# Sliding-window attention with a mixture of attention experts: a mask added by TensorE, loads in halves, expert outputs turned by transfers, and a new list of steps

## The chip, the cores and the metric

The kernel runs on one core of one Trainium2 chip. The metric is the device time of one execution in microseconds (us). Of three runs of the kernel before, the median is 242.83 us (240.96 to 242.97).

## The reference

```python
# attention: B=8 batches, H=8 heads, S=576 positions, D=64
scores = scale * np.matmul(q, k.transpose(0, 1, 3, 2))
mask = np.abs(pos[:, None] - pos[None, :]) <= 32
attn_out = softmax(np.where(mask, scores, -1e9)) @ v
x = attn_out.transpose(0, 2, 1, 3).reshape(B, S, 512)
# mixture: E=4 experts, Hd=64, the best two by gate for each position
logits = x @ w_gate                      # softmax weights w over the best two
for e in range(4):
    q, k, v = x @ wq[e], x @ wk[e], x @ wv[e]
    a = softmax(where(causal, -1e9, scale * q @ k.T))
    ye = a @ v @ wo[e]
    out += (w of e, or 0) * ye
```

All inputs and the output are float32.

## The kernel before

Everything is written as short steps, and the string `ORDER` lists them in the order in which they are issued. A step's name is an operation, then its batch `b` and further digits; `:a`, `:v`, `:g` name the engine of a copy (ScalarE = ACT, VectorE = DVE, GpSimd = POOL), `@` the PSUM banks. Each engine runs its instructions strictly in that order, and waits by semaphores for what another engine or a transfer delivers. Nothing is scheduled at run time, so the list decides what stands behind what. There are three buffers (`NAT`) for loaded q and k tiles, two for v and two for the transposed tiles of each group.

Attention, for each batch and each group `g` of four heads:

- `lq`, `lk` load q and k, `lv` loads v, all from the queue of SyncE (SP), except q or k steps marked `:f`, which ACT issues. Each load carries a dependency on the last TensorE (PE) instruction that stands before it in the list (`load`), so it isn't issued before that one is done.
- `tq`, `tk` turn q and k by 32 x 32 blocks on DVE (`turn`); `vc` copies v into the second alignment that the windows need.
- `sc` computes half of the windowed scores (columns 0 to 287 or 288 to 575), each 64 keys against the queries of their window, in blocks `BLK`; `ex` takes the exponential from PSUM into `A` (ACT).
- `mk` multiplies `A` by the 0/1 band `MASK`, so that what lies outside the window is 0. All 64 are on POOL.
- `av` multiplies by v, with a column of ones for the sums; `un` divides (reciprocal and multiply on DVE) into `XN`.

Mixture, for each batch:

- `xt` turns `XN` on PE by an identity matrix, `xf` copies it out of PSUM, `xb` casts to bf16.
- `ga`, `gt`, `ge`, `gm`, `gu` compute the gate and the weights of the best two experts.
- `pp`, `pe` project to q and k of a pair `j` of experts, `pv`, `ve` to v.
- `ps`, `xe`, `se` compute the causal scores by chunks 0 to 3 (`CHUNKS`), their exponential (ACT) into `ATE`, and the causal zeroes on the diagonal blocks (POOL).
- `po` multiplies by v, `oe` scales by gate and sum (DVE) into `OE`.
- `pt` turns `OE` on PE: five matmuls of 128 x 128 with the bf16 identity, into a bank; `ot` copies the bank to `OTT`.
- `py` multiplies `OTT` by the output weights, `ye` copies to `Y`, `st` stores.

`zz` steps are four matmuls of zeroes that keep PE running. `s_` steps set constants up. `cw` and `lw` load and cast weights.

The program runs batch `b`'s mixture among batch `b+1`'s and `b+2`'s attention. In line L179 (`mm`) stand all matmuls, in L182 (`turn_pe`) all of PE's turns, in L171 and L173 (`copy`) all copies, in L294 the DVE turns, in L339 `ex`, in L343 `mk`, in L513 and L515 `xe`, in L518 `se`, in L551 to L553 `oe`, in L185 the loads.

Of the kernel before, what the change touches and what calls it, by code (L numbers as in the profile page):

```python
# [24 lines left out]
NOE = 2  # L25

ORDER = """
    lq011:f lq012:e lk011:e lk012:e s_warm tq011:e tq012:e tk011:e lq000:e s_ones lk000:e s_zero tk012:e tq000:e
# [4 lines left out]
    av03@4 ex1011@2 lw11 mk1011:g cw10:g av04@0 lk200:e un03@4 un04@0 lq200:e xt00@2 tq110:e xf00:a@2 xt02@0 xt01@4
    sc111@62 xf02:a@0 mk1010:g xf01:a@4 xb01:g xb02:g lv10 tk200:e xb00:a cw00:a ex1110@6 sc110@04 ex1101@4 cw11:g
    lv13 ex1111@2 pp000@6 pp001@4 lw01 pe000:a@6 mk1101:g mk1111:g mk1000:g pe001:v@4 ex1100@0 pp011@2 tq200:e lv14
    ps001@6 lw2 xe001@6 ps002@0 ga0@4 xe002@0 sc200@60 pe011:a@2 lq210:e cw01:a pp010@2 gt0@4 ge0@4 vc11:g gm0@4
    mk1110:g gu0@4 av13@4 lv20 vc10:a lv23 ex2000@6 av12@6 ex2001@0 pe010:v@2 un13@4 ps013@2 xe013@2 mk1100:g cw2:g
    ps010@0 ps000@4 av10@2 xe010@0 av11@0 lk210:e xe000@4 pv01@4 un12@6 un10@2 ve01:a@4 ps003@6 av14@5 xe003@6 ps011@2
    xe011@2 lk300:e un11@0 ps012@0 xt11@6 xf11:a@6 un14@5 xt10@4 tq210:e xf10:a@4 xe012@0 sc201@26 tk210:e mk2001:g
    se002 se003 se001 xb11:g mk2000:g lv21 ex2011@6 lv22 lq300:e ex2010@2 xb10:g pv00@4 xt12@0 xf12:v@0 ve00:a@4  # L40
    sc211@62 sc210@04 mk2010:g se012 tk300:e lq310:e se010 mk2011:g ex2111@2 xb12:a lk310:e ga1@2 ex2110@6 ex2100@0
    pv10@6 gt1@2 ge1@2 pp101@0 lv24 ex2101@4 gm1@2 pp110@4 pe110:a@4 gu1@2 ve10:a@6 lv33 tq300:e pp111@2 mk2110:g
    mk2111:g pe111:a@2 pp100@4 pe101:v@0 lv34 lv32 sc300@06 pe100:a@4 vc21:g tk310:e vc20:g pv11@2 av23@4 ex3000@0 lw3
    av22@0 mk2100:g ex3001@6 mk2101:g av24@3 un23@4 un22@0 un24@3 ps103@6 ve11:a@2 se000 po00@4 ps113@0 oe00@4 xe103@6
    xe113@0 ps110@6 xe110@6 lk400:e ps102@2 xt21@0 xe102@2 pt00@4 ot00:a@4 xt22@5 tq310:e av20@6 un20@6 av21@2
    xf21:a@0 ps111@0 xf22:a@5 sc301@46 un21@2 xe111@0 ex3010@4 lq400:e sc311@20 ex3011@6 ex3111@0 xt20@4 mk3000:g
    se011 ex3110@2 se102 xb21:g se113 lv31 se013 tk400:e cw3:g xb22:g mk3010:g mk3001:g ps100@6 xf20:a@4 lk410:e
    ps101@0 xe100@6 zz4@2 po01@2 lq410:e oe01@2 xe101@0 sc310@46 ex3101@6 xb20:g se100 se103 ex3100@4 ps112@0 pp211@2
    xe112@0 pp201@6 lq500:e lv30 se101 tq400:e pt01@0 po10@4 pe211:a@2 pp210@2 ot01:v@0 pp200@0 pe201:v@6 oe10@4
    vc30:g se110 mk3110:g mk3011:g mk3111:g pe200:a@0 mk3100:g sc401@64 pe210:v@2 lk510:e sc400@20 lk500:e ex4011@4  # L50
    ex4001@0 ex4000@2 pv20@4 mk3101:g ps201@0 ex4010@6 vc31:g se112 mk4010:g tk410:e ps202@2 xe201@0 xe202@2 tq410:e
    ve20:v@4 ga2@6 gt2@6 ge2@6 av34@7 un34@7 ps212@0 xe212@0 lv44 gm2@6 py01@4 xt32@7 lv43 gu2@6 ye01:a@4 pv21@0
    ve21:a@0 xf32:v@7 av32@2 un32@2 py02@1 lv42 ye02:a@1 av33@4 lq510:e av31@6 un33@4 ps203@0 ps200@2 xe203@0 xe200@2
    un31@6 tk500:e xt31@4 xf31:a@4 sc411@06 xb32:g mk4000:g mk4001:g mk4011:g lv52 se203 av30@2 un30@2 ex4111@6 lv41
    sc410@46 xt30@2 xb31:a se111 ex4110@0 ex4101@6 tq500:e ex4100@4 py00@0 mk4100:g mk4110:g xf30:a@2 st01 lv40 po11@6
    ye00:a@0 lv50 sc500@42 xb30:a ex5001@2 mk4101:g vc40:g ga3@0 lv54 oe11@6 ex5000@4 ps213@6 xe213@6 lq600:e ps210@2
    tq510:e ps211@4 lv51 pt10@1 xe210@2 xe211@4 pp300@6 gt3@0 vc41:g pe300:a@6 pp301@2 tk510:e ge3@0 mk4111:g
    pe301:a@2 sc501@46 ex5010@4 gm3@0 av40@2 lq610:e gu3@0 un40@2 ex5011@6 ot10:a@1 av42@4 av43@6 un42@4 av41@0
    ps300@2 ps302@4 un43@6 st00 lk600:e xe300@2 lv53 xt41@6 un41@0 xe302@4 pt11@0 xf41:v@6 xt40@2 mk5011:g xf40:a@2
    ot11:a@0 av44@1 un44@1 sc510@46 se201 se213 mk5000:g sc511@20 lk610:e se210 se212 mk5010:g se202 mk5001:g se211  # L60
    ex5101@6 ex5100@4 py10@6 mk5100:g se300 xb40:g tk600:e se200 ex5110@2 py11@4 lk710:e ye10:a@6 lk700:e po21@2
    xt42@6 ex5111@0 xf42:a@6 pv30@0 ye11:a@4 tq600:e pp310@6 oe21@2 tk610:e xb42:a ve30:a@0 po20@4 oe20@4 xb41:a
    mk5111:g mk5110:g mk5101:g pe310:a@6 vc51:g sc600@20 ex6000@2 ex6001@0 tq610:e pp311@6 pp401@2 pe311:a@6 ps303@4
    ps312@0 xe312@0 xe303@4 st02 lv60 av54@6 vc50:g ga4@7 lv64 ps313@0 un54@6 pe401:a@2 ps311@4 ps301@2 py12@6 gt4@7
    xe313@0 xe311@4 lv62 st10 av50@0 ye12:v@6 st12 lv63 av52@4 xe301@2 un50@0 lv61 pv31@6 ge4@7 sc601@20 un52@4
    pp400@4 lq700:e ex6010@2 gm4@7 ex6011@0 pe400:a@4 ve31:v@6 pp410@2 ps403@0 gu4@7 lv72 ps400@6 se312 xe403@0
    ps401@4 xe400@6 av51@0 un51@0 lv71 pe410:a@2 av53@6 un53@6 ps310@2 tk700:e xe401@4 xt50@0 xt51@4 xe310@2 xt52@2
    xf50:a@0 xf52:v@2 pt21@3 pp411@6 xf51:a@4 ot21:v@3 lq710:e sc610@04 pe411:v@6 xb50:a xb51:a ps402@2 mk6011:g se303
    mk6000:g se302 se301 xb52:g pp501@6 ex6100@0 ex6101@4 pe501:a@6 pp500@0 se313 se311 se310 tq700:e pt20@4 pe500:a@0
    po31@6 ot20:a@4 xe402@2 mk6010:g oe31@6 lv70 po30@0 vc61:g ps413@4 lv73 xe413@4 ps412@2 xe412@2 vc60:a oe30@0  # L70
    sc611@64 tk710:e tq710:e mk6101:g mk6001:g pp510@2 ex6111@4 ex6110@6 pe510:a@2 pv40@0 ps502@4 mk6100:g mk6111:g
    mk6110:g xe502@4 sc701@62 ve40:v@0 ex7010@6 ex7011@2 av61@4 av63@6 py22@0 pv51@1 un61@4 un63@6 ve51:a@1 av60@2
    av62@4 ye22:a@0 ps411@6 un60@2 un62@4 ps410@0 ga5@2 gt5@2 st11 av64@3 un64@3 ps503@4 xe411@6 xe410@0 lv74 ps500@6
    xe503@4 pp511@0 ge5@2 xe500@6 pe511:a@0 py21@4 ye21:a@4 sc700@60 gm5@2 gu5@2 ex7000@6 ex7001@0 se411 sc711@24
    xt61@6 xf61:v@6 pt31@0 ot31:v@0 xt62@1 ex7111@4 se500 se412 ex7110@2 xt60@4 xf62:a@1 xf60:a@4 pv41@1 ve41:v@1
    sc710@26 mk7000:g se402 se410 se400 se401 xb61:g se403 py20@4 ye20:v@4 mk7111:g po40@0 st20 st21 st22 vc70:a
    ex7100@2 pt30@2 se413 mk7100:g mk7010:g ex7101@6 mk7101:g se503 xb60:g ps511@6 ps513@4 ga6@3 oe40@0 xb62:a xe511@6
    gt6@3 ps501@0 xe513@4 ps510@6 po41@4 xe501@0 ot30:v@2 pt40@2 xe510@6 pv50@0 oe41@4 pt41@4 pp611@6 ge6@3 gm6@3
    ot41:v@4 pp600@4 pe611:v@6 pe600:v@4 ve50:a@0 se510 se501 pp610@0 py31@6 mk7001:g se502 ot40:a@2 ye31:a@6 pp601@4
    pe610:v@0 gu6@3 po50@0 pe601:a@4 oe50@0 ps602@2 ps512@6 vc71:g mk7011:g xe512@6 av71@4 un71@4 av70@0 st31 ps601@6  # L80
    un70@0 se511 mk7110:g av74@4 un74@4 xe602@2 se512 se513 xe601@6 ps610@2 ps611@0 xe610@2 pv61@5 av73@6 un73@6
    xe611@0 py32@4 xt70@2 py30@0 po51@6 ye32:a@4 ye30:a@0 xt72@4 xf70:v@2 ve61:v@5 xf72:a@4 st32 ps612@2 oe51@6 py42@5
    av72@0 ps600@6 xe612@2 ye42:v@5 un72@0 xe600@6 ps613@4 xb72:a xe613@4 py41@2 ye41:v@2 st30 xt71@0 se610 xf71:a@0
    st41 pv60@6 xb70:g se600 se601 xb71:g py40@2 ps603@0 ve60:a@6 xe603@0 pp710@4 pe710:v@4 pt51@0 ye40:v@2 se602
    se603 ot51:a@0 pt50@1 ot50:a@1 po60@6 se611 pp711@4 st42 se613 se612 po61@0 pe711:a@4 ps713@2 ps712@4 oe60@6
# [557 lines left out]
```

## Time and profile before

| | |
|---|---|
| median of 3 runs | 242.83 us |
| profiled execution, its own time | 242.79 us |
| its span | 240.7 us |
| PE busy | 214.6 us |
| DVE busy | 170.4 us |
| POOL busy | 157.4 us |
| ACT busy | 155.1 us |
| mean of all transfers | 169 GB/s |

The span is from the first to the last profiled instruction of the execution. Busy time is the time in which at least one instruction of an engine ran. PE's busy time is not the same as PE at its peak, since the ends of pipelined matmuls are modelled. The chain of waits follows the work that ended last back to the start. A window's row gives its length, busy time and instruction count of PE, PE's weight loads, DVE, ACT and POOL, the granted clock, the share of the transfer engines and GB/s. A group's row gives busy time and mean nanoseconds of one, and then the idle time before it with what ended it. A float32 matmul or weight load leaves two records in the trace.

### The profile page before, as it was taken

The page shows a single profiled execution, that of the slowest core. Times are in us where ns is not written, and L with a number is a line of the kernel's source. Part 1 is how long each engine was busy: PE and PEld are TensorE (multiplying, and loading weights), DVE is VectorE, ACT ScalarE, POOL GpSimd, SP SyncE. Part 2 cuts the span into 40 slices and gives each one's busy share as a digit, 9 for nine tenths or more (in the row PEclk, how much of TensorE's full clock was granted, in tenths as well). Part 3 has the DMA queues.
Part 4 walks back from the last instruction along what each step waited for, and adds up shares of the span by engine and source line. Part 5 has one row for each costly group of instructions (what it writes and reads, how often), then busy time and mean ns, then how long its engine had stood idle before and what let it go on. Part 6 is the DMA issues. An engine that isn't in the chain of part 4 may idle for free.

```text
span 240.7 us, 12380 instructions
## 1 busy us (share of the span) xinstructions
PE 214.6 (89%) x5542; PEld 172.7 (72%) x5556; DVE 170.4 (71%) x351; ACT 155.1 (64%) x241; POOL 157.4 (65%) x193
## 2 busy tenths in 40 slices
PE   0496688899999899999899998999999999999980
PEld 0463576688888688688697976887978878786650
DVE  2967584878789669886976986669845766847660
ACT  2045346958476683869757874998588647757841
POOL 7069948956994899685969962499039993250500
PEclk9999999999999999999999999999999999999997
DMA  6696799766966286578685829826010510332375
GB/s 226 264 229 158 139 255 262 176 173 207 319 147 198 87 260 167 201 191 218 155 245 162 300 51 250 205 101 177 5 26 3 200 58 35 112 112 92 108 283 197
DMA packets 55157, 40.65 MB, mean 169 GB/s; under 512 B 45376, under 2 KB 46400, under 8 KB 55104
## 3 DMA queue, kind: packets, MB, share of 16 engines
q1 hardware_dynamic: 54960, 39.57, 56.7%
q8 instruction: 43, 0.70, 1.2%
q10 hardware_dynamic: 144, 0.29, 0.4%
q14 instruction: 10, 0.08, 0.1%
HBM read 30.42 MB, written 9.44 MB: 166 GB/s over the span
## 4 chain that ended last, share of the span: by engine, by line
PE 81%; DVE 8%; DMA 4%; issue 3%; ACT 2%; ACTq 0%; DVEq 0%
PE PS L179 72%; PE PS L182 8%; DMA kn<-in_k_dram 3%; DVE Tkn L294 3%; DVE Tqn L294 2%; DMA qn<-in_q_dram 2%; ACT ATE L513 1%; DVE OE L553 1%; DVE XN L371 1%; DVE PS L551 0%; DVE RC L370 0%; DVE QKE L173 0%; ACT Y L171 0%; DVE RG L552 0%; ACTq L638 0%
## 5 line engine op out<-in xcount | busy, mean ns | idle before, releaser
L343 POOL TENSOR_TENSOR A<-A,MASKP 128x576 f32<-128x576 f32 x64 | 89.3, 1411 | 24.4 <-ACT A L339 23.8
L179 PE MATMUL PS<-Tqn,Tkn 32*64 32x128 f32 (+3 forms) x2560 | 46.9, 277 | 16.0 <-DVE Tkn L294 11.2
L179 PEld LDWEIGHTS PS<-Tqn,Tkn 32*64 32x64 f32 x2560 | 40.7, 135 | 22.6 <-DVE Tkn L294 12.2
L339 ACT ACTIVATE A<-PS 128x576 f32<-128x576 f32 x64 | 38.6, 651 | 28.2 <-PE PS L179 25.8
L513 ACT ACTIVATE ATE<-PS 128x1024 bf16<-128x1024 f32 x48 | 47.5, 1026 | 11.0 <-PE PS L179 10.9
L518 POOL TENSOR_SCALAR_AFFINE_SELECT ATE<-ATE 128x256 bf16<-128x256 bf16 (+1 forms) x80 | 29.0, 382 | 28.2 <-ACT ATE L513 17.1
L294 DVE STREAM_TRANSPOSE Tkn<-kn 128x576 f32<-128x576 f32 (+1 forms) x34 | 37.3, 1176 | 8.5 <-DMA kn<-in_k_dram 6.8
L294 DVE STREAM_TRANSPOSE Tqn<-qn 128x576 f32<-128x576 f32 (+1 forms) x34 | 37.2, 1176 | 7.0 <-DMA qn<-in_q_dram 4.6
L179 PE MATMUL PS<-V,A 128*64 128x65 f32 (+1 forms) x1280 | 38.5, 222 | 0.6 <-ACT V L171 0.4
L179 PEld LDWEIGHTS PS<-V,A 128*64 128x64 f32 (+1 forms) x1280 | 35.9, 132 | 3.3 <-issue 1.0
L371 DVE TENSOR_TENSOR XN<-PS,RC 128x512 f32<-128x512 f32 x32 | 22.1, 691 | 1.1
L173 POOL CAST XTB<-XTF 128x1024 bf16<-128x1024 f32 (+1 forms) x18 | 12.4, 704 | 15.5 <-DVE XTF L173 8.4
L173 POOL COPY V<-V 64x2048 f32<-64x2048 f32 (+1 forms) x12 | 21.0, 1749 | 0.8 <-issue 0.2
L179 PE MATMUL PS<-WO,OTT 128*128 128x512 bf16 (+1 forms) x85 | 18.9, 342 | 0.9 <-DVE OTT L173 0.3
L171 ACT COPY XTF<-PS 128x1024 f32<-128x1024 f32 (+1 forms) x23 | 14.9, 699 | 6.9 <-PE PS L182 6.7
L182 PE MATMUL PS<-ident,XN 128*128 128x128 f32 x144 | 19.3, 277 | 0.0
L179 PE MATMUL PS<-WV,XTB 128*128 128x256 bf16 (+1 forms) x192 | 18.6, 256 | 0.2 <-ACT ATE L513 0.2
L171 ACT CAST QKE<-PS 128x576 bf16<-128x576 f32 x21 | 13.4, 643 | 7.5 <-PE PS L179 7.5
L179 PE MATMUL PS<-XTB,WK 128*128 128x288 bf16 x128 | 18.0, 286 | 0.1
L179 PE MATMUL PS<-QKE 64*128 64x64 bf16 (+4 forms) x192 | 17.0, 278 | 1.1 <-DVE QKE L173 1.1
L171 ACT COPY Y<-PS 128x1024 f32<-128x1024 f32 (+2 forms) x16 | 12.2, 778 | 8.8 <-PE PS L179 8.8
L179 PE MATMUL PS<-XTB,WQ 128*128 128x288 bf16 x128 | 17.9, 286 | 0.0
(71 smaller groups left out, 264.1 us busy)
## 6 DMA issues: line engine op xcount, KB each, us to landing
qn<-in_q_dram SPq DMA_DIRECT2D x15, 576.0 KB, 4.7
kn<-in_k_dram SPq DMA_DIRECT2D x15, 576.0 KB, 4.9
V<-in_v_dram SPq DMA_DIRECT2D x32, 256.0 KB, 4.3
out_dram<-Y SPq DMA_DIRECT2D x14, 512.0 KB, 3.4
V<-in_v_dram SPq DMA_DIRECT2D x8, 128.0 KB, 3.3
out_dram<-Y SPq DMA_DIRECT2D x16, 64.0 KB, 2.3
out_dram<-Y SPq DMA_DIRECT2D x4, 256.0 KB, 2.5
kn<-in_k_dram SPq DMA_DIRECT2D x2, 288.0 KB, 4.2
```

The costliest lines, as they stand in the source:

```text
L171: nc.scalar.copy(o, i)
L173: eng(c).tensor_copy(o, i)
L179: last_pe[0] = nc.tensor.matmul(*a, **kw)
L182: last_pe[0] = nc.tensor.transpose(*a)
L294: nc.vector.transpose(T[:, :].rearrange("q (p o) -> q o p", o=18)[:, o0:o1], n_[:, o0:o1, 32 * dh:32 * dh + 32])
L339: nc.scalar.activation(AT[(2 * b + g) % NAT_][half][p], two(b0)[:, :, 0:HS], EXP, scale=scale_att)
L343: eng(c).tensor_tensor(out=ap, in0=ap, in1=MASK[:, None, HS * half:HS * half + HS].to_broadcast([128, 2, HS]), op=MULT)
L371: nc.vector.tensor_tensor(out=XN[T // 2][:, T % 2, :].rearrange("p (g h d) -> p g h d", g=2, h=4), in0=u[:, :, :, 0:64], in1=rc[:, :, :, N ...
L513: nc.scalar.activation(chunk(A, ch), two(b0), EXP, scale=scale_moe)
L518: nc.gpsimd.affine_select(ap, ap, pattern=[[0, n], [1, w]], compare_op=IS_GE, fill=0.0, base=0, channel_multiplier=-1)
L553: nc.vector.tensor_tensor(out=O[:, :, :, :].rearrange("p t e d -> p e t d"), in0=p_[:, :, :, 0:64], in1=rg[:, :, :, None].to_broadcast([12 ...
```

## The change

- **Mask of batch 0.** For the two groups of batch 0 (`BAND`), `sc` begins with four matmuls of 128 x 288 that write `ident_bf` times `NB` into the four banks, where `NB` is 0 in the band and -8.0e9 outside; the scores are added to it, and the exponential then gives 0 outside. The eight `mk` steps of batch 0 are gone. `s_band` makes `NB` on POOL, and `s_mask` makes the 0/1 mask from it by one comparison. Of the other 56 `mk`, five (of batch 1) are on DVE.
- **Loads in halves.** A q or k load of part 3 or 4 brings two of the four heads: 64 partitions, 288 KB. All whole loads of q and k are replaced by two such; the turns on DVE stay whole. SP's list of transfers grows from 115 to 158, the fourteen of the next point included.
- **Expert outputs turned by transfers.** For batches 0 to 6 `pt` and `ot` give way to `dt`, a transposing transfer from `OE` to `OTT` that SP issues. Batch 7 keeps `pt` and `ot`. There are four buffers `OE` in place of two.
- **The last 64 queries of the experts** (chunk 3) are computed for both pairs of experts in one `ps`, one exponential and one `se`, into new tiles `AT3`.
- `lw3` is one load in place of two.
- **The list of steps** is new throughout.

```diff
-NOE = 2
+NOE = 4
 ...
-    lq011:f lq012:e lk011:e lk012:e s_warm tq011:e tq012:e tk011:e lq000:e s_ones lk000:e s_zero tk012:e tq000:e
-    lq100:e sc011@02 lk100:e lv03 tk000:e s_pads sc010@46 ex0111@2 lv01 lv00 ex0100@4 zz0@2 s_mask zz3@2 ex0101@6
-    sc000@24 s_ident ex0110@0 mk0111:g ex0001@4 lv02 lwg sc001@06 tq100:e tk100:e mk0101:g mk0110:g zz1@4 ex0011@6
-    ex0000@2 zz2@4 lk110:e lw10 lv12 lv04 mk0001:g mk0100:g mk0011:g ex0010@0 tk110:e vc00:a sc100@46 sc101@02 lq110:e
-    lw00 ex1000@4 vc01:g ex1001@6 mk0000:g av00@4 ex1010@0 un00@4 av01@6 lv11 mk0010:g av02@0 mk1001:g un01@6 un02@0
 ...
+    lq003:e lq004:e s_zero tq000:e s_ones s_warm lk004:e lk003:e s_band lk104:e s_ident lq012:f lk012:e tk000:e lv02
+    zz4@0 zz3@0 lq011:e lk011:e zz2@0 lv01 tk012:e s_pads tq012:e sc000@02 ex0001@2 lv03 lv00 lk103:e sc001@46
+    ex0000@0 tq011:e tk011:e lq114:e s_mask vc00:g vc01:g tk100:e sc011@02 ex0011@6 ex0010@4 lq113:e lv04 lk204:e
+    lk113:e sc010@46 ex0100@4 ex0101@6 ex0111@2 lk114:e av00@4 lw11 tq110:e un00@4 av01@6 ex0110@0 un01@6 av03@2 lw00
+    lq104:e av04@0 lq103:e lw2 un04@0 av02@4 tk110:e xt00@6 xf00:a@6 sc111@06 un02@4 lw01 un03@2 xt01@4 xb00:g cw11:g
+    ex1110@0 zz0@0 ex1111@6 cw00:a xf01:a@4 xb01:g lq204:e xt02@0 lq203:e lw10 tq100:e xf02:v@0 sc100@26 sc101@40
+    ex1001@6 ex1011@0 mk1111:v mk1011:v tq200:e ex1010@4 lk203:e xb02:g cw10:g ex1000@2 cw01:a pp011@6 lv13 pe011:a@6
+    lk214:e sc110@04 ex1100@0 pp000@2 ex1101@4 lv12 lv11 pp001@6 tk200:e mk1100:v cw2:g pv00@0 pe000:a@2 pe001:a@6
+    lv10 ps001@2 xe001@2 lk213:e sc201@46 ex2010@4 pp010@2 mk1101:g mk1010:g ve00:v@0 lv14 mk1001:v mk1110:g mk1000:v
 ...
+    st40 ps711@6 ye50:a@2 po61@2 xe73@4 ps702@4 oe60@0 ps712@0 xe711@6 oe61@2 ga7@6 st50 xe702@4 gt7@6 pv71@7 xe712@0
+    ve71:v@7 ps701@2 ps710@4 ge7@6 pv70@0 xe710@4 ve70:v@0 gm7@6 ps700@4 xe701@2 st51 dt60 dt61 py52@7 ye52:a@7
+    xe700@4 se702 se712 se711 se701 py61@2 se710 se73 po71@0 st52 gu7@6 py60@4 oe71@0 se700 ye61:a@2 ye60:a@4 st61
 ...
+    BAND = ((0, 0), (0, 1),)
+    FAR = -8.0e9
 ...
-    ATE = many(3, [128, 3264], BF16, "ATE")
+    ATE = many(3, [128, 3136], BF16, "ATE")
+    AT3 = many(2, [128, 320], BF16, "AT3")
 ...
+    NB = sb.tile([128, SP_], BF16, name="NB")
 ...
     def s_mask():
+        nc.gpsimd.tensor_scalar(out=MASKP, in0=NB, scalar1=0.0, scalar2=None, op0=IS_GE)
 ...
+        if part > 2:
+            h = 2 * (part - 3)
+            load(t[32 * h:32 * h + 64, :, :].rearrange("p o d -> p (o d)"),
+                 src[b, 4 * g + h:4 * g + h + 2].rearrange("h (p o) d -> (h p) (o d)", o=18), queue)
 ...
+        band = (b, g) in BAND
+        if band:
+            for hh in range(4):
+                mm(PS[:, bank[hh], 0:HS], ident_bf, NB[:, 32 + c0:32 + c0 + HS], start=True, stop=False, skip_group_check=True)
 ...
-                   start=(dh == 0), stop=(dh == 1), skip_group_check=True)
+                   start=(dh == 0 and not band), stop=(dh == 1), skip_group_check=True)
 ...
+    def ps(c, b, *at):
+        if len(at) == 2:
+            for j in range(2):
+                keys(b, j, [(4, 512, 576, 64 * j)], at[1])
+        else:
+            keys(b, at[0], CHUNKS[at[1]], at[2])
 ...
+    def xe(c, b, *at):
+        if len(at) == 2:
+            nc.scalar.activation(AT3[b % 2][:, 0:256].rearrange("p (j e c) -> p e j c", j=2, e=2),
+                                 two(at[1])[:, :, 0:128].rearrange("p e (j c) -> p e j c", j=2), EXP, scale=scale_moe)
 ...
+    def dt(c, b, j):
+        nc.sync.dma_start_transpose(OTT[b % 2][:, j, :].rearrange("p (t k) -> p t k", k=128),
+                                    OE[(2 * b + j) % NOE][:, :, :, :].rearrange("p t e d -> p (t e d)"))
```

More of the change, by code (lines that the diff above doesn't have):

```diff
@@ L24 @@
 NAT_ = 3
-NOE = 2
+NOE = 4
 ORDER = """
-    lq011:f lq012:e lk011:e lk012:e s_warm tq011:e tq012:e tk011:e lq000:e s_ones lk000:e s_zero tk012:e tq000:e
-    lq100:e sc011@02 lk100:e lv03 tk000:e s_pads sc010@46 ex0111@2 lv01 lv00 ex0100@4 zz0@2 s_mask zz3@2 ex0101@6
-    sc000@24 s_ident ex0110@0 mk0111:g ex0001@4 lv02 lwg sc001@06 tq100:e tk100:e mk0101:g mk0110:g zz1@4 ex0011@6
-    ex0000@2 zz2@4 lk110:e lw10 lv12 lv04 mk0001:g mk0100:g mk0011:g ex0010@0 tk110:e vc00:a sc100@46 sc101@02 lq110:e
-    lw00 ex1000@4 vc01:g ex1001@6 mk0000:g av00@4 ex1010@0 un00@4 av01@6 lv11 mk0010:g av02@0 mk1001:g un01@6 un02@0
[L33 to L85, printed above, removed]
-    ps711@6 xe713@2 pp700@2 oe61@0 xe712@4 pp701@0 pe700:v@2 pv71@2 ve71:v@2 xe711@6 st40 py52@3 pt61@4 ye52:v@3 st52
-    py51@6 pe701:a@0 ot61:a@4 ps703@0 ye51:v@6 xe703@0 ps702@2 st51 xe702@2 ps701@4 se703 ga7@0 se702 gt7@0 ps700@6
-    ps710@2 xe701@4 xe700@6 se711 se700 pt60@1 se713 ge7@0 se701 se712 xe710@2 se710 gm7@0 py50@4 pv70@6 ot60:a@1
-    ve70:a@6 gu7@0 py61@2 py62@0 ye62:a@0 ye61:a@2 ye50:v@4 po70@4 oe70@4 po71@6 oe71@6 py60@0 pt70@2 ot70:v@2 pt71@3
-    ot71:v@3 py72@2 st50 py710@3 st62 py711@4 st61 ye72:v@2 ye60:a@0 st60 ye710:a@3 st72 ye711:v@4 py701@2 st710 st711
-    py700@3 ye701:a@2 st701 ye700:a@3 st700
@@ L249, in lw3 @@
     def lw3():
-        for eo in range(2):
-            load(WST[3][64 * eo:64 * eo + 64, :].rearrange("p (j x) -> p j x", x=512),
-                 moe_wo.rearrange("(j o) d x -> o d j x", o=2)[eo])
+        load(WST[3].rearrange("p (j x) -> p j x", x=512), moe_wo.rearrange("(j o) d x -> (o d) j x", o=2))
     def cw(c, n, j):
```

119 lines of the change are left out of this document (83 added, 36 removed).

## The prediction, made before the changed kernel ran

> **What bounds the kernel now.** I read the page first: its busy shares and its chain.
>
> ```profile
> PE 214.6 (89%) x5542; PEld 172.7 (72%) x5556; DVE 170.4 (71%) x351; ACT 155.1 (64%) x241; POOL 157.4 (65%) x193
> PE 81%; DVE 8%; DMA 4%; issue 3%; ACT 2%; ACTq 0%; DVEq 0%
> PE PS L179 72%; PE PS L182 8%; DMA kn<-in_k_dram 3%; DVE Tkn L294 3%; DVE Tqn L294 2%; DMA qn<-in_q_dram 2%; ACT ATE L513 1%; DVE OE L553 1%; DVE XN L371 1%; DVE PS L551 0%; DVE RC L370 0%; DVE QKE L173 0%; ACT Y L171 0%; DVE RG L552 0%; ACTq L638 0%
> ```
>
> TensorE (PE) is busy 89% of the span and is 81% of the chain; ScalarE (ACT) is 2% of it and GpSimd (POOL) is not on it. Where PE is not busy, the windows say.
>
> ```profile
> 0.00:6.00 6.00, 0.00 (x0) 0.00 (x0) 1.38 (x3) 1.49 (x2) 4.59 (x15) 1.00 0.69 227
> 6.00:12.00 6.00, 2.84 (x108) 2.64 (x113) 6.00 (x12) 0.25 (x1) 0.00 (x0) 1.00 0.65 265
> 12.00:18.00 6.00, 5.78 (x200) 4.12 (x197) 3.83 (x19) 2.44 (x5) 4.18 (x3) 1.00 1.01 226
> 18.00:24.00 6.00, 3.94 (x139) 2.38 (x127) 4.50 (x4) 3.56 (x5) 5.51 (x4) 1.00 0.69 159
> 24.00:30.00 6.00, 3.78 (x179) 3.42 (x163) 3.21 (x4) 2.38 (x4) 5.46 (x5) 1.00 0.78 138
> ...
> 78.00:84.00 6.00, 5.18 (x198) 4.09 (x194) 3.90 (x5) 4.12 (x9) 4.89 (x8) 1.00 0.25 70
> ...
> 114.00:120.00 6.00, 5.24 (x116) 3.69 (x113) 5.86 (x11) 4.50 (x8) 5.86 (x5) 1.00 0.63 146
> ...
> 144.00:150.00 6.00, 5.19 (x161) 4.44 (x157) 3.95 (x15) 3.10 (x6) 0.84 (x1) 1.00 0.84 228
> ```
>
> The second and third numbers of a row are its length and PE's busy time. The first 30 us lose much (the first 6 whole, 3.16 us between 6 and 12, 2.06 and 2.22 between 18 and 30: 13.7 with the 0.2 between); after that only three windows lose over 0.7 us: 0.82, 0.76 and 0.81, together 2.4. The granted clock is 1.00. So three things can move the end: PE's own work, the start, and those 2.4 us.
>
> **The turns of the expert outputs** (`pt`, `ot`). Fourteen of the sixteen leave PE for transfers `dt`; batch 7 keeps its two.
>
> ```profile
> L182 PE MATMUL PS<-ident_bf,OE 128*128 128x128 bf16 x80 | 7.0, 220 | 0.5 <-DVE OE L553 0.5
> 89.72 0.28 PE PS L182 x5
> ```
>
> Eighty matmuls are 7.0 us busy, so a turn of five is 0.44, and 14 are 6.1: the upper bound, since the end of one overlaps the next step. The chain shows one turn as 0.28 us: 14 are 3.9. I take the middle, **-5.0**. The copies `ot` that go with them, eight on ACT and six on DVE, are covered by PE's other steps (ACT is 2% of the chain) and count nothing.
>
> What the transfers cost: the trace has none of their kind. One moves 160 KB. The nearest rows are the landings.
>
> ```profile
> DMA packets 55157, 40.65 MB, mean 169 GB/s; under 512 B 45376, under 2 KB 46400, under 8 KB 55104
> V<-in_v_dram SPq DMA_DIRECT2D x32, 256.0 KB, 4.3
> out_dram<-Y SPq DMA_DIRECT2D x16, 64.0 KB, 2.3
> Y<-in_moe_wk_dram SPq DMA_DIRECT2D x2, 256.0 KB, 4.4
> kn<-in_k_dram SPq DMA_DIRECT2D x2, 288.0 KB, 4.2
> ATE<-in_moe_wo_dram SPq DMA_DIRECT2D x2, 256.0 KB, 4.1
> 32.69 6.47 DMA kn<-in_k_dram
> ```
>
> The bounds are 2.3 us (the smallest store) and 6.47 us (the slowest load on the chain); I take 4.3, the load of V, whose 256 B pieces are most of the packets under 512 B. Who waits: `py` of the same batch. In the new list there are ten and more PE steps between `dt` and `py`, save for batch 6, where after `oe61` ACT still does four exponentials before the bank of `py61` is free.
>
> ```profile
> L513 ACT ACTIVATE ATE<-PS 128x1024 bf16<-128x1024 f32 x48 | 47.5, 1026 | 11.0 <-PE PS L179 10.9
> SPq L185 <- PE PS L179: 116.3, 50, 12.0
> ```
>
> Four of 1.03 us cover 4.1; a second `dt` is issued some 0.4 later, so it lands 4.7 after `oe61`: +0.6 late, between 0 and 2.8; I take **+0.4**, since `dt60` starts before `oe61`. On SP `dt` stands ahead of loads and stores and waits there for `oe`; SP's own waiting for PE was 116.3 us, and that is the cover of this and of the 43 further issues (115 become 158).
>
> [...]
>
> **The mask of batch 0.** Eight of 64 multiplies leave POOL and five of batch 1 go to DVE.
>
> ```profile
> L343 POOL TENSOR_TENSOR A<-A,MASKP 128x576 f32<-128x576 f32 x64 | 89.3, 1411 | 24.4 <-ACT A L339 23.8
> L179 PE MATMUL PS<-XTB,WQ 128*128 128x288 bf16 x128 | 17.9, 286 | 0.0
> ```
>
> POOL is freed of 13 x 1.41 = 18.3 us; it is not on the chain, so this counts in the start alone. PE gets 16 matmuls of 288 columns; a projection of that shape is 17.9 / 128 = 0.14 us, so 2.2 us in all. The first twelve are issued while PE waits for K and Q (below); the last four, of `sc010`, show: **+0.5** (0 to 2.2).
>
> **The start, step by step.**
>
> ```profile
> 0.81 0.38 SPq L185 DMA_DIRECT2D qn<-in_q_dram  x1
> 4.62 2.34 DVE L294 STREAM_TRANSPOSE Tqn<-qn 128x288 f32<-128x288 f32 x4 [4.62 <-DMA qn<-in_q_dram]
> 9.16 4.49 PE L179 MATMUL PS<-Tqn,Tkn 32*64 32x64 f32 x160 [9.16 <-DVE Tkn L294]
> 9.48 2.32 DVE L294 STREAM_TRANSPOSE Tqn<-qn 128x576 f32<-128x576 f32 x2
> 13.92 0.17 DVE L224 MEMSET XTF<- 128x128 f32 x1
> 16.07 0.17 DVE L235 MEMSET WG<- 128x128 f32 x1
> 16.25 2.51 PE L179 MATMUL PS<-Tqn,Tkn 32*64 32x96 f32 x160
> 27.80 3.96 PE L179 MATMUL PS<-V,A 128*64 128x65 f32 x128
> 47.05 0.44 issue
> L339 ACT ACTIVATE A<-PS 128x576 f32<-128x576 f32 x64 | 38.6, 651 | 28.2 <-PE PS L179 25.8 <-issue 1.5 <-POOL A L343 0.7
> L371 DVE TENSOR_TENSOR XN<-PS,RC 128x512 f32<-128x512 f32 x32 | 22.1, 691 | 1.1
> L179 PE MATMUL PS<-WV,XTB 128*128 128x256 bf16 x128 | 15.3, 273 | 0.0
> ```
>
> Before: q lands at 4.60, DVE turns eight half tiles, scores begin at 9.16; a pair of `sc` is 160 records, 4.49 us then and 2.51 at 16.25. After: `tq000` is a whole tile and needs both halves, the second issued 0.4 later, some 5.3. Then 2.3 for q, 0.2 of memsets, 2.3 for k: `sc000` at 10.2, with two transfers' worth of bytes per tile as before. At the slow pace it ends at 12.4, `sc001` at 14.0. `sc011` waits for DVE: four pairs of half tiles, 1.17 a pair (2.34 for two), and the memsets (13.92 to 16.24, 2.3) make 10.2 + 4.7 + 2.3 = 17.2. `sc011` and `sc010` at a pace between the two end at 20.5, two exponentials of 0.65 later `av00` starts: **21.8 against 27.80**. But by 27.80 the old list had also done `sc100` and most of `sc101`.
>
> Then DVE's order bites. `un00` stands behind `tq110`, whose second load (`lq113`) is asked for only after `sc011` (19.0) and lands some 4.2 later: 23.2, turned at 25.5, `un00` (0.69 and a reciprocal) at 26.4, and PE's `av02` waits for its bank. `un01` and `un04` follow, `tk110` ends at 30.2 and `sc111` waits for it; `un02`, `un03`, `tq100`: 34.4, and `sc100` waits. From there PE has two `sc` (2.5), four `pp` (17.9 / 16 = 1.1 each), two `sc` (2.5), `pv00` (15.3 / 8 = 1.9) and one `ps` (some 0.6): 11.9, that is 46.3 with 9 `sc`, 5 `av`, 3 `xt`, 4 `pp`. The old list reaches the same count at 47.05 (the chain's issue gap), with `ga0` and `ps002` in place of `pv00`. I take **-0.5**, between -6 (nearly half of the 13.7 us lost up to 30 us, if loads and un-steps come as soon as their data) and +4 (one further load landing late on DVE's order).
>
> [...]
>
> **The rest.** `ps`, `xe`, `se` of the last 64 queries are done for both pairs of experts at once: PE's matmuls stay, eight exponentials of ACT go; 0. `lw3` in one load: 0. The new list also redeals copies among ACT, DVE and POOL; POOL and ACT carry less than before and DVE about as much, so of the 2.4 us that PE loses later I take back **-1.0** (0 to -2.4; to +3 if the new order brings waits of its own).
>
> **Sum**, against the profiled execution's own 242.79 us (span 240.7 and 2.1 around it; the median of the runs is 242.83): -5.0 + 0.4 + 0.5 - 0.5 - 1.0 = -5.6: **237.2 us**. This forecast's own range is 234 to 240.
>
> **The rivals.**
> A. The start gains more: the mask's absence lets un-steps follow at once. For it: POOL's 24.4 us of idle ahead of masks and the lost PE time up to 30 us. Against: DVE's order above. With -6 in place of -0.5: 231.7.
> B. Loads come late through the split: each half is tied to a place in PE's list, and the second is asked for a step later, as `lq113`. DVE's turns wait in order, and all un-steps behind them. Against: 116.3 us of slack on SP. At the start alone +4: 241; with some 0.7 us for each later batch, 246.
> C. The other side: the transfers that turn are slow. V's loads move 256 B pieces, 1024 to a load, in 4.3 us against 2.3 for the smallest store, so 2.0 us per 1024 pieces. If a turn writes 32 B pieces it has 5120: 10 us, and lands 12 us after its issue. Two in a row land some 22 us after `oe61` with 4.1 covered, on the ring that also carries the loads: 237.2 + 16 to 18, less what stays hidden in other steps, 250. It decides from a landing of about 7 us on. [...]
> D. PE's freed 5 us become waits, because the end is set by the engines that feed it (DVE 71%): 242. Against it speaks DVE's 8% of the chain.
>
> **How the numbers follow.** Forecast 0.46, A 0.16, B 0.14, C 0.16, D 0.08. The measurement tells about 1% apart, 2.4 us: below 240.4 lie the forecast and A nearly whole, 0.60; above 245.3 lie C and most of B, 0.26; the rest, D and the smaller B, 0.14. The range runs from below A's 231.7 to B's worse end: 230 to 247, and leaves out C's far end and a start better than A.
>
> **What would show it.** Right: PE's L182 group on OE at 10 matmuls; `av` starting near 22 us; `dt` landing in 3 to 6 us, with PE not waiting on a transfer before `py`; no window after 48 us that loses over 1 us. Wrong: `py` waiting for OTT, landings of `dt` above 7 us, K and Q loads growing over 5 us, or DVE waiting for q and k in every batch.

## The result, and the profile after

The changed kernel takes 253.36 us, the median of four runs (250.39 to 255.97), against 242.61 us for the kernel before (240.96 to 242.97): a ratio of 1.0375, with an interval of 1.0268 to 1.0481. It is slower by some 9 us, where I had forecast 5.6 us faster, and it lies above my range. Times here are medians of all runs of a kernel, while ratios, and differences taken from them, leave out executions in a slower state, as two of these four were (254.38 us and the profiled one). The profiled execution is the longest of the four (255.97 us, span 254.2), so its lines show the loss some 5 us too large.

The page of the changed kernel: busy times, chain by engine, the queue that carries nearly all transfers (packets, MB, share of 16 engines' span), and the issues with their median time to landing.

```profile
PE 220.9 (87%) x5490; PEld 174.5 (69%) x5502; DVE 170.1 (67%) x350; ACT 148.6 (58%) x219; POOL 145.6 (57%) x181
...
q1 hardware_dynamic: 64832, 41.86, 74.8%
...
PE 67%; DMA 11%; DVE 10%; issue 7%; ACT 2%; POOL 1%; SPq 0%; DVEq 0%; POOLq 0%; ACTq 0%
...
kn<-in_k_dram SPq DMA_DIRECT2D x32, 288.0 KB, 5.7
qn<-in_q_dram SPq DMA_DIRECT2D x31, 288.0 KB, 5.0
V<-in_v_dram SPq DMA_DIRECT2D x32, 256.0 KB, 4.4
...
OTT<-OE SPq DMA_TRANSPOSE x14, 3.8
```

Before, transfers were 4% of the chain; now they are 11%. A half of a q or k tile is 288 KB and takes 5.0 to 5.7 us to land, longer than the whole 576 KB tile did before:

```profile
qn<-in_q_dram SPq DMA_DIRECT2D x15, 576.0 KB, 4.7
kn<-in_k_dram SPq DMA_DIRECT2D x15, 576.0 KB, 4.9
```

That was on the prediction's list of what would show it wrong. The transfers that turn the expert outputs land in 3.8 us in the median, as expected (the longest in 7.2).

Where PE loses its time, in windows of 6 us of the changed kernel (length, busy time of PE, PEld, DVE, ACT, POOL with their counts, granted clock, share of the DMA engines, GB/s), and what the engines waited for (us, times, longest):

```profile
6.00:12.00 6.00, 0.78 (x20) 0.39 (x17) 4.28 (x6) 0.00 (x0) 1.43 (x1) 0.95 1.03 216
12.00:18.00 6.00, 5.76 (x166) 4.17 (x151) 5.61 (x27) 1.25 (x3) 0.00 (x0) 0.50 1.09 256
...
36.00:42.00 6.00, 4.29 (x162) 3.63 (x163) 3.28 (x5) 1.40 (x3) 2.10 (x3) 0.73 1.05 194
...
66.00:72.00 6.00, 2.19 (x77) 1.89 (x77) 3.40 (x4) 1.05 (x1) 3.93 (x6) 0.79 0.71 108
...
108.00:114.00 6.00, 3.63 (x71) 2.73 (x71) 2.10 (x4) 1.94 (x2) 2.39 (x7) 0.72 1.00 169
```

```profile
POOL V L175 <- DMA V<-in_v_dram: 21.2, 6, 11.2
DVE Tqn L303 <- DMA qn<-in_q_dram: 12.4, 6, 6.5
...
DVE Tkn L303 <- DMA kn<-in_k_dram: 6.6, 5, 2.2
```

Read the windows from the right: in four of the five rows the DMA engines are fully busy (a share of 1.0 and above) while only 169 to 256 GB/s move. Of all windows of 6 us, twelve have a share of 1.00 or more here, and two in the kernel before (1.01 at 226 and 1.02 at 257 GB/s). That points to engines that are occupied with too little to show for it, rather than to loads that are asked for late; the experiments decide. DVE now waits 19.0 us for q and k where the kernel before had 11.4, and POOL 21.2 us for v, which stands behind them on the same queue. The waits before:

```profile
DVE Tkn L294 <- DMA kn<-in_k_dram: 6.8, 3, 3.6
...
DVE Tqn L294 <- DMA qn<-in_q_dram: 4.6, 1, 4.6
```

### The profile page after: what moved, and what is told of

Same layout as the page of the kernel before. It is cut to its first block, busy times and chain, and to the rows that moved or that the text cites. A ratio compares the mean times of both kernels' runs of the same rounds, so it can differ in the third digit from the quotient of the medians.

```text
span 254.2 us, 12335 instructions
## 1 busy us (share of the span) xinstructions
PE 220.9 (87%) x5490; PEld 174.5 (69%) x5502; DVE 170.1 (67%) x350; ACT 148.6 (58%) x219; POOL 145.6 (57%) x181
## 3 DMA queue, kind: packets, MB, share of 16 engines
q1 hardware_dynamic: 64832, 41.86, 74.8%
## 4 chain that ended last, share of the span: by engine, by line
PE 67%; DMA 11%; DVE 10%; issue 7%; ACT 2%; POOL 1%; SPq 0%; DVEq 0%; POOLq 0%; ACTq 0%
PE PS L181 62%; PE PS L184 6%; DMA qn<-in_q_dram 5%; DVE Tkn L303 3%; DVE Tqn L303 3%; DMA kn<-in_k_dram 2%; DMA V<-in_v_dram 2%; DMA out_dram<-Y 1%; DMA OTT<-OE 1%; ACT A L352 1%; DVE XN L384 1%; POOL V L175 1%; DVE Y L175 0%; ACT Y L173 0%; DVE OE L569 0%
## 5 line engine op out<-in xcount | busy, mean ns | idle before, releaser
L356 POOL TENSOR_TENSOR A<-A,MASKP 128x576 f32<-128x576 f32 x51 | 71.8, 1424 | 4.4 <-ACT A L352 4.1
L181 PE MATMUL PS<-Tqn,Tkn 32*64 32x128 f32 (+3 forms) x2560 | 49.2, 287 | 16.2 <-issue 6.1
L181 PEld LDWEIGHTS PS<-Tqn,Tkn 32*64 32x64 f32 x2560 | 42.5, 141 | 23.2 <-issue 9.6
L181 PE MATMUL PS<-V,A 128*64 128x65 f32 (+1 forms) x1280 | 40.7, 225 | 3.6 <-issue 1.3
L532 POOL TENSOR_SCALAR_AFFINE_SELECT ATE<-ATE 128x256 bf16<-128x256 bf16 x64 | 24.9, 409 | 32.6 <-ACT ATE L529 32.4
L181 PEld LDWEIGHTS PS<-V,A 128*64 128x64 f32 (+1 forms) x1280 | 36.9, 133 | 7.6 <-issue 2.7
L175 POOL CAST XTB<-XTF 128x1024 bf16<-128x1024 f32 (+1 forms) x26 | 18.1, 715 | 30.5 <-ACT XTF L173 26.5
L175 POOL COPY V<-V 64x1536 f32<-64x1536 f32 (+1 forms) x12 | 20.2, 1680 | 22.1 <-DMA V<-in_v_dram 21.2
L173 ACT COPY Y<-PS 128x1024 f32<-128x1024 f32 (+2 forms) x22 | 17.6, 805 | 8.2 <-PE PS L181 6.3
L184 PEld LDWEIGHTS PS<-ident,XN 128*128 128x128 f32 x144 | 15.7, 140 | 2.5 <-issue 1.3
```

The source lines that it names most:

```text
L173: nc.scalar.copy(o, i)
L175: eng(c).tensor_copy(o, i)
L181: last_pe[0] = nc.tensor.matmul(*a, **kw)
L184: last_pe[0] = nc.tensor.transpose(*a)
L356: eng(c).tensor_tensor(out=ap, in0=ap, in1=MASK[:, None, HS * half:HS * half + HS].to_broadcast([128, 2, HS]), op=MULT)
L532: nc.gpsimd.affine_select(ap, ap, pattern=[[0, n], [1, w]], compare_op=IS_GE, fill=0.0, base=0, channel_multiplier=-1)
```

## The experiments

My theory after the result: a transfer to 64 partitions moves at about half the rate, and that alone is the loss. The rivals: the new list is worse (in particular the place of each half), or the transfers that turn are.

**e1: halves by columns.** The same number of loads, of the same size, at the same places; each now covers all 128 partitions and half of the columns.

```diff
-            h = 2 * (part - 3)
-            load(t[32 * h:32 * h + 64, :, :]..., src[b, 4 * g + h:4 * g + h + 2]..., queue)
+            o0, o1 = ((0, 9), (9, 18))[part - 3]
+            load(t[:, o0:o1, :]..., src[b, 4 * g:4 * g + 4]...[:, o0:o1, :]..., queue)
```

> The changed kernel with the same number of q and k loads at the same places and of the same 288 KB, but each brings half of the columns of all 128 partitions in place of all columns of 64 partitions. Theory H (a load to 64 partitions moves at about half the rate, so loads fill the queue and come late): the share of the transfer engines falls from 74.8% to about 60%, the landings of q and k from 5.0 to 5.7 us to under 4.5, and the time to 238 to 244 us. Rival T (the 14 turning transfers clog the queue): the time stays within 2 us of the changed kernel's 250 to 252. Rival L (the new order of steps itself costs it): landings get shorter, yet the time stays above 247.

Measured: 237.02 us (236.18 to 237.52), ratio to before 0.9809 (0.9737 to 0.9881). The page and the chain's first load of this kernel:

```profile
PE 215.7 (92%) x5490; PEld 171.1 (73%) x5502; DVE 169.7 (72%) x350; ACT 148.3 (63%) x219; POOL 145.4 (62%) x181
...
q1 hardware_dynamic: 68672, 41.86, 67.7%
...
kn<-in_k_dram SPq DMA_DIRECT2D x32, 288.0 KB, 4.5
qn<-in_q_dram SPq DMA_DIRECT2D x31, 288.0 KB, 3.9
```

```profile
1.26 4.17 DMA qn<-in_q_dram
```

With more packets (68672 against 64832) and the same 41.86 MB, the DMA engines are busy for 160 us (67.7% of 235.7) instead of 190 (74.8% of 254.2); I had expected a share of 60%, and a time at least 1 us longer. No window of 12 us has a share above 0.94; the changed kernel has two, with 1.15 (24 to 36 us) and 1.12 (132 to 144). The shape of the halves is therefore the whole loss and more: without it the change is 2% faster than before, within 0.2 us of my forecast. This version, called the columns kernel from here on, beats both kernels.

Where the loss sits is read from e13 below, which has most of it and whose profile is not of a long execution. Of the 10.1 us between its span and this one, 7.8 are idle time of PE (27.8 against 20.0) and 2.3 are matmuls taking longer (218.0 us busy against 215.7), at a lower granted clock (0.983 against 0.993). The profile of the changed kernel has 13.3 and 5.2.

**e2 and e11: one whole load per tile**, at the place of the first half, or at that of the second.

```diff
- ... lq003:e lq004:e ...
+ ... lq000:e ...
```

> The changed kernel with one whole load of 128 partitions in place of each pair of halves, at the place of the first of the two. Theory H: 238 to 244 us, as with the halves by columns. A rival to the shape of the loads, that their number and their ties to PE's list matter (60 loads, each asked for separately): this one gains clearly more than the halves by columns, by 3 us or more. Rival T: 249 or more.

> The changed kernel with one whole 576 KB load per tile at the place of the second half's load, where e2 had it at the place of the first. Theory (what e2 lost against the columns kernel is that a whole load at the early place goes ahead of transfers that are needed sooner): 236 to 239 us. Rival (two smaller loads let other transfers pass between them, and one 576 KB load holds them up wherever it stands): 241 to 244 us. Third case: the data now comes too late for its tile, and DVE waits for q and k: over 244 us.

Measured: 242.45 us, ratio 1.0013 (0.9963 to 1.0063), and 242.72 us, ratio 1.0003 (0.9955 to 1.0050). Both are 2% above the columns kernel, so neither place suits a whole load; for e11 that is the rival's case.

**e15: both column halves at the first place.**

> The columns kernel with both halves issued one behind the other at the first half's place. Theory (whole loads at either place gave 242.5 us because one load of 576 KB is tied to one place; spreading a tile over two places is what gains): 241 to 243 us. Rival (pieces of 288 KB let other transfers between them, wherever they stand): 236 to 239 us.

Measured: 240.51 us, ratio 0.9942 (0.9893 to 0.9990), between the two cases. Smaller pieces seem to help somewhat, and spreading them over two places too; the intervals don't let me share out the 5 us more finely.

**e3 and e8: the loads alone, in the kernel before.** Each whole load becomes two, first by partitions, then by columns.

> The kernel before with each of its 30 whole q and k loads as two loads of 64 partitions at the same place; nothing else. Theory H: 4608-byte packets go from about 0.18 to 0.3 us, the share of the transfer engines from 57% to about 68%, and the time from 242.6 to 246 to 252 us, lost ahead of 48 us. Rivals T and L: within 1.5 us of the kernel before.

> The kernel before with each whole q and k load as two of half the columns at the same place. Theory H: 64-partition pieces were what cost 2.1% in the other split, so here the time is within 1% of the kernel before (240 to 244 us). If the second issue and the number of loads cost: 245 us or more.

Measured: 248.26 us, ratio 1.0207 (1.0105 to 1.0309), by partitions; 240.82 us, ratio 0.9960 (0.9906 to 1.0014), by columns. So a second issue for each tile costs nothing that can be measured, and the shape costs 5 to 6 us here too: 5.0 against the kernel before, 6.0 against halves by columns.

**e5: transfers by themselves.** Eight tiles in each phase, all issued in a row, with nothing else running.

> Transfers alone, none of the computation: 4.7 MB of q and k into eight tiles five times, each time as eight whole loads (128 partitions), as sixteen of 64 partitions, as sixteen of half the columns of 128 partitions, as sixteen of 64 partitions with the upper half from a second queue, and as eight whole loads with four turning transfers among them; then four turning transfers alone. Theory H (64 partitions take in half of what 128 do): phases 1 and 3 last about 12 us, phase 2 about 21 to 24 us, and phase 4, where both halves are under way at once, about 12 to 15. If instead the number of transfers is what costs, phases 2 and 3 are equal. For the turns: if they hold the other transfers up, phase 5 lasts more than 3 us longer than phase 1; otherwise less than 2 us longer.

The timeline of DVE, which reads one element of each tile as it lands (start, us); four tiles of the whole loads, then four of the 64-partition halves; and the windows of three phases: whole, 64-partition halves, halves by columns.

```profile
8.17 0.18 DVE L28 TENSOR_TENSOR ACC<-ACC,T 128x16 f32<-128x16 f32 x1 [2.27 <-DMA T<-in_q_dram]
9.61 0.18 DVE L28 TENSOR_TENSOR ACC<-ACC,T 128x16 f32<-128x16 f32 x1 [1.27 <-DMA T<-in_q_dram]
...
20.85 0.17 DVE L28 TENSOR_TENSOR ACC<-ACC,T 128x16 f32<-128x16 f32 x1 [3.94 <-DMA T<-in_q_dram]
23.43 0.17 DVE L28 TENSOR_TENSOR ACC<-ACC,T 128x16 f32<-128x16 f32 x1 [2.40 <-DMA T<-in_q_dram]
```

```profile
2.00:14.00 12.00, 3.42 (x11) 0.00 (x0) 1.00 0.97 384
18.00:37.00 19.00, 1.23 (x7) 0.00 (x0) 1.00 1.03 233
41.00:54.00 13.00, 1.23 (x7) 0.00 (x0) 1.00 0.95 342
```

A 576 KB tile follows the last one after 1.4 us when it is loaded whole (8.17 to 9.61) and after 2.6 us in 64-partition halves (20.85 to 23.43). In both phases the DMA engines are shown as fully busy (0.97 and 1.03), at 384 and 233 GB/s. From the first issue to the last read, the eight tiles took 14.5 us whole (0.73 to 15.24), 22.9 in 64-partition halves (15.74 to 38.66) and 16.1 in halves by columns (39.07 to 55.18). With the upper halves from a second queue they took 20.6 (55.68 to 76.25); I had expected 12 to 15, so two halves under way at once don't make up for each other. With four turning transfers among the whole loads it was 15.9 (76.75 to 92.67), 1.4 more than without: the turns don't hold the loads up.

The rate in 64-partition halves is 0.61 of the rate of whole loads (233 against 384 GB/s). What limits it no run here shows.

**e13 and e14: where the loss arises.** Halves by partitions from batch 2 on only (24 of 32 tiles), or in batches 0 and 1 only; the others by columns. The expectations say 8 tiles for the second, but q and k of batch 0's second group are halves by columns in every kernel here (`lq011`, `lq012`), so it is 6, and the changed kernel has 30 tiles by partitions, not 32.

```diff
-        if part > 2:
+        if part > 2 and b < 2:      # e14: b >= 2
             # by columns
+        elif part > 2:
+            # by partitions
```

> The changed kernel with q and k of batches 0 and 1 in halves by columns (8 of 32 tiles) and the halves by partitions from batch 2 on (24 tiles). Theory (PE's remaining work at 72 us was 14 us behind the columns kernel, so the slow transfers hurt where nothing is loaded ahead yet): 238 to 242 us. Rival (each slow tile costs alike, and 24 of 32 tiles carry three quarters of the 15 us): 247 to 250 us.

> The opposite: batches 0 and 1 in halves by partitions, columns from batch 2 on. Theory (the crowded start): 246 to 250 us. Rival (alike for each tile): 240 to 242 us.

Measured: e13 249.07 us (four runs, 246.79 to 254.53), ratio 1.0228 (from two runs, without an interval); e14 242.39 us, ratio 1.0027 (0.9987 to 1.0067). Against the columns kernel (0.9809) that is 10.1 us for 24 tiles and 5.3 for 6, or 0.4 and 0.9 us per tile. My theory of a crowded start is wrong: two thirds of the loss come after it. But the rival, that each tile costs alike, isn't right either, since a tile of the start seems to cost about twice as much. In e5 a tile cost 1.2 us more of the queue; a third of that reaches the end later on, and three quarters in the start.

**e4, e7 and e12: the turns in the old list.** e4 is the kernel before with `dt` in place of `pt` and `ot` for batches 0 to 6, and four `OE` buffers; e7 has the buffers alone; e12 has all three parts (turns, band, halves by columns) in the old list.

> The kernel before with the turns of the expert outputs of batches 0 to 6 by transfers at the places of the old turns, and four buffers for them; no other part of the change. Theory H, under which the term of the prediction for these turns stands: 5 us less of PE's work, some of it lost to later arrival: 237 to 242 us, landings 3 to 5 us. Rival T: 246 us or more, with py waiting for the turned tile. If PE's freed time turns into waits for other engines: 241 to 244.

> The kernel before with four buffers for the expert outputs in place of two, and nothing else: a control for the run with the turns by transfer, since the tiles behind these buffers lie at other addresses. If the 1.0% came from the transfers: within 0.5% of the kernel before. If it came from the places of the tiles: slower by about 1% too.

> All three parts of the change in the old list: turns of batches 0 to 6 by transfers, the band on TensorE, and loads in two halves by columns. Theory (the parts bring nothing by themselves, and the 5 us of the columns kernel come from the new list): the single readings added, minus 0.4% for columns and plus 1.0% for the turns, 243 to 245 us. Rival (the parts help each other, because smaller loads let the turns through): 238 to 241 us.

Measured: e4 244.65 us, ratio 1.0099 (1.0046 to 1.0152); e7 241.96, ratio 0.9993 (0.9948 to 1.0038); e12 243.19, ratio 1.0018 (0.9971 to 1.0065). In the old list the transfers gain nothing and may cost 1%; e4 lies by the upper end of the case in which freed time turns into waits (241 to 244 us), and below rival T. The readings of e4, e8 and e9 (below) would add to 1.5%; the 0.2% of e12 is less, but the intervals are too wide to call that a help.

**e6: turns back on PE in the new list.** In the columns kernel, `pt` and `ot` stand in free banks at the places of `dt`.

> The changed kernel with loads by columns (237.0 us), and the turns of the expert outputs back on PE with their copies, at the places of the transfers, into banks that are free there. If PE's 5 us of the prediction's term are real in this order: 240 to 244 us. If the turns by transfer cost as much as they free, as the kernel before with them alone (1.0% longer) suggests: 234 to 238.

Measured: 258.95 us, ratio 1.0690 (1.0593 to 1.0786). Both cases of the expectation were far off. This doesn't price PE's time: the inserted copies stand in the queues of ACT and DVE where nothing was planned for them, and PE stands behind them. Its waits for the copies themselves are 5.3 of the 12 us that PE is idle longer than in the columns kernel (32.0 against 20.0). The waits of e6:

```profile
DVE OTT L176 <- PE PS L185: 11.3, 6, 4.2
PE PS L182 <- DVE OTT L176: 5.3, 5, 2.9
```

**e16, e17 and e18: PE's time alone.** Five turns of the identity, which nobody reads, beside each of the fourteen turns; no copy, and no wait for an expert output.

```diff
+    def px(c, b, j, b0):
+        o = one(b0).bitcast(BF16)
+        for t in range(NQT):
+            turn_pe(o[:, 128 * t:128 * t + 128], ident_bf, ident_bf)
```

> The columns kernel (237.0 us), which keeps its fourteen transfers, with five turns of the identity on TensorE beside each of them, into a bank that is free there; nobody reads them. They put back the TensorE time that the change takes off and nothing else (no copies, no wait for an expert output). Theory (TensorE is the bound, and the prediction's term of 5.0 us stands): 241 to 243 us. Rival (TensorE has waits there that take the turns in): 237 to 239 us.

> The kernel before with the same dummy turns in the bank of each pt of batches 0 to 6, ahead of it, so the turns of these batches are doubled on TensorE. Theory (5.0 us for fourteen turns): 246 to 248 us. Rival (hidden in waits): 242 to 244 us.

> The e4 kernel (old list, turns of batches 0 to 6 by transfers, 244.65 us) with the dummy turns in the places and banks where the turns stood. Against before it has the transfers in place of the copies ot, and the same TensorE work. Theory (TensorE's 5 us were gained in e4 and the transfers lost 7): 248 to 251 us. Rival (in the old list TensorE's time at these places is worth nothing, and the transfers cost 2 us): 244 to 246 us.

Measured: e16 242.95 us, ratio 1.0037 (1.0002 to 1.0072); e17 246.89, ratio 1.0211 (1.0148 to 1.0274); e18 243.09, ratio 1.0019 (0.9973 to 1.0065). In the columns kernel and in the kernel before, seventy turns on PE are worth 2.3% (1.0037 against 0.9809, some 5.5 us) and 2.1% (5.1 us). In the old list with transfers they are worth nothing: e18 is no slower than e4, and faster than both cases of its expectation. The busy lines of e4 and then of e18:

```profile
PE 212.9 (89%) x5472; PEld 170.6 (71%) x5486; DVE 168.9 (70%) x346; ACT 149.9 (62%) x232; POOL 157.3 (66%) x193
```

```profile
PE 215.1 (89%) x5542; PEld 174.1 (72%) x5556; DVE 169.2 (70%) x346; ACT 150.2 (62%) x232; POOL 157.5 (65%) x193
```

PE is busy 2.2 us longer in e18, and the spans are 239.9 and 240.5 us: the freed time seems to have turned into waits of PE. Which wait took it over I could not settle. And since e18 has the transfers and the PE work of the kernel before, and its time (1.0019), the 1% of e4 is not shown to be the transfers' price.

**e9 and e10: the band.** e9 adds it to the kernel before. e10 takes it out of the columns kernel, with batch 0's masks multiplied on POOL again.

> The kernel before, with nothing changed but the first batch's mask: TensorE adds the band in front of the scores of batch 0, the eight mask multiplications of batch 0 are gone, and the steps that build the band and the identity stand after the warm-up. Theory (the prediction's two terms for the start and the band, half a microsecond each way, cancel where the list stays as it was): within 1% of before, 241 to 244 us. Rival: building the band on GpSimd that early holds up what GpSimd does next, or the start was bound by the masks all along: over 245 or under 240 us.

> The changed kernel with halves by columns (237.0 us), with batch 0's masks multiplied on GpSimd again and no band on TensorE. Theory (the start gains by its order, the band is only worth the eight masks that no longer stand between exponential and product): 1 to 4 us slower than the columns kernel, 238 to 241 us. Rival 1: the band is a cost that the rest hides; without it 236 us or less. Rival 2: the new list stands on the band, and the start falls back by the whole queue of masks: 243 us or more.

Measured: e9 244.34 us, ratio 1.0087 (1.0047 to 1.0127); e10 243.39, ratio 1.0096 (1.0047 to 1.0144). The band by itself makes the old list 0.9% slower: in e9 the first scores start at 9.32 us and the first `av` at 26.46, where the kernel before has them at 9.16 and 27.80, so little is gained there, PE has the band's sixteen matmuls more, and later waits take the rest. Without it the new list loses 2.9% (1.0096 against 0.9809, some 7 us), as rival 2 had it. The chain of e10 shows where (start, us, what):

```profile
15.81 1.47 POOL V L176
...
17.32 1.90 POOL V L176
...
19.30 5.52 POOL A L358 x4
...
24.87 4.19 PE PS L182 x72
```

The new list has the first copies of v on POOL. With the masks there too, four of them stand behind those copies, and PE gets on only at 24.87 us. A list planned without the band would not have to stand so; that was not tried.

## Why the prediction was wrong, by its own steps

**The loads in halves** are the step that failed. The sum has no term for them: in the rows of the kernel before, a 64-partition load of 256 KB (`moe_wo`) lands in 4.1 us, no later than a 128-partition one (`moe_wk`, 4.4), and I took that for their price. They cost some 14 us (1.0375 against 0.9809). The row was right and the wrong kind of row: the landing of one load says little of the rate of many. In e5 the first whole tile is there at most 3.8 us after its issue (0.73 to 4.57), and each of the last ones 1.4 us after the one before; in 64-partition halves that is 5.1 us (15.74 to 20.85), and then 2.6. With the 1.2 us more per tile, the 30 tiles would have been a bound of 36 us that my range didn't hold.

Nor do the halves gain anything when nothing else runs: in e5 eight tiles take 22.9 us in them, against 14.5 whole.

**Rival B** had the direction, "loads come late through the split", but its mechanism was the place of the second half and its price at most +9 over the forecast. The same halves at the same places, cut by columns, are the fastest kernel here, so the places are not the loss and the shape is.

**The turns, -5.0.** The matmul group on `OE` fell to 10, as the prediction said. This is the line of the changed kernel:

```profile
L184 PE MATMUL PS<-ident_bf,OE 128*128 128x128 bf16 x10 | 0.9, 220 | 0.8 <-DVE OE L569 0.8
```

e16 measures the term at 5.5 us in the list that the change has. In the old list the term would have been wrong (e4, e18): there it looks like rival D, PE's freed time turning into waits.

**The arrival of `dt`, +0.4.** The landing was taken as 4.3 us and measured 3.8. A second one I took as issued 0.4 us after the first, as loads are; SP needs 1.2 us to issue a turning transfer (a median of 1.23). PE's waits for it in the changed kernel, and the one place where it is on the chain, batch 6, where I had looked for it (0 to 2.8 us allowed):

```profile
PEld L181 <- DMA OTT<-OE: 0.8, 2, 0.4
...
PE PS L181 <- DMA OTT<-OE: 0.3, 1, 0.3
```

```profile
237.98 2.90 DMA OTT<-OE
```

Waits of 0.3 to 0.8 us: the size was right. Rival C, slow turns, fell. Its pieces of 32 B aren't what is moved: e4's page has 9408 packets under 512 B more than the kernel before (54784 against 45376), 672 for each of its fourteen transfers of 160 KB, or some 240 B to a packet.

**The start, -0.5, and the band, +0.5.** The walk by hand holds where the halves don't disturb it. PE's first `av` (`V,A`) and its last `pp` of batch 0 (`XTB,WQ`) in the columns kernel, and the latter in the changed one:

```profile
20.69 2.20 PE L181 MATMUL PS<-V,A 128*64 128x65 f32 x66 [0.73 <-ACT A L353]
...
43.51 1.15 PE L181 MATMUL PS<-XTB,WQ 128*128 128x288 bf16 x8
```

```profile
49.81 1.15 PE L181 MATMUL PS<-XTB,WQ 128*128 128x288 bf16 x8
```

I had 21.8 for the start of the one and 46.3 for the end of the other; the columns kernel has 20.69 and 44.66. The changed kernel is 6 us behind it, and it begins with its very first loads: the chain shows the first q landing at 7.6 us, where I had worked out 5.3.

```profile
1.43 6.13 DMA qn<-in_q_dram
...
10.28 3.42 DVE Tkn L303 x4
```

How little the start changes in the sum is seen from the work left at 72 us. The windows from 72 us to the end, PE busy first: before, columns kernel, e10, changed kernel.

```profile
72.00:260.00 188.00, 158.73 (x3890) 127.03 (x3898) 119.41 (x250) 116.94 (x180) 104.60 (x136) 0.98 0.45 135
```

```profile
72.00:260.00 188.00, 152.91 (x3763) 122.91 (x3772) 114.20 (x241) 112.40 (x163) 106.53 (x135) 0.99 0.57 144
```

```profile
72.00:260.00 188.00, 158.49 (x3973) 126.74 (x3971) 116.69 (x244) 115.47 (x169) 110.44 (x138) 0.99 0.56 147
```

```profile
72.00:260.00 188.00, 166.94 (x4048) 133.48 (x4054) 121.73 (x261) 120.56 (x176) 113.90 (x140) 0.98 0.67 155
```

The columns kernel has 5.8 us less left than before, and that is about the seventy turns (6.1 us busy), all of which come after 72 us: so its start gains about nothing, as -0.5 and +0.5 said. One profile tells this to a few us only: e7, the kernel before but for two more buffers, has 161.17 us left at 72 and the same span of 240.7. And the zero is two large numbers, not two small ones: without the band (e10) the start is 5.6 us behind. I had priced the band as 2.2 us of matmuls and not asked what the new list does to POOL without it. The matmuls themselves are 3.6 us in the columns kernel:

```profile
L181 PE MATMUL PS<-NB,ident_bf 128*128 128x288 bf16 x16 | 3.6, 362 | 0.0
```

**The later losses, -1.0.** The prediction read only three windows after 30 us that lose over 0.7 us, 2.4 together. Short of the last 7 us, it passed over three more, with 0.94, 0.88 and 0.90, so it had 5.1 to take from:

```profile
36.00:42.00 6.00, 5.06 (x160) 4.08 (x143) 2.82 (x3) 4.30 (x7) 5.32 (x7) 1.00 0.89 261
42.00:48.00 6.00, 5.12 (x143) 3.85 (x145) 5.00 (x15) 5.41 (x8) 5.86 (x5) 1.00 0.76 173
...
228.00:234.00 6.00, 5.10 (x86) 3.42 (x86) 3.60 (x9) 2.62 (x5) 0.00 (x0) 1.00 0.71 258
```

From 72 us on PE is idle for 10.8 us in the columns kernel (235.7 - 72 - 152.91) and for 10.0 before: +0.8 instead of -1.0. So that the columns kernel lies within 0.2 us of the forecast is in part luck: its terms are off by about 1 us on either side, and the profiles fix them no better than that. It holds only for the list as a whole: its three parts in the old list (e12) gain nothing, and the joint step for the last 64 queries and the single `lw3`, both priced at 0, were not tried by themselves.

## What to carry to other kernels

When a transfer is split, split it so that each piece still covers all 128 partitions: here the same halves cost nothing by columns, and 5 us (old list) to some 14 us (new list) by partitions. Price loads that come in a row by bytes over the rate of their shape (in e5 384 GB/s whole, 233 in 64-partition halves), not by the landing time of one load. A DMA share near 1.0 beside a low GB/s is a hint of it in the windows, but not a proof: the columns kernel too has a fortieth of its span with a share of 0.9 or more at 161 GB/s (88.4 to 94.3 us; the first turning transfer is issued at 89.0). A part of a change that was planned together with its list of steps has no price of its own: the band and the transfers gained nothing in the old list, while in the new one the band is worth 7 us, and the PE time that the transfers free 5.5.
